# Seven half-size block products instead of eight for the two products with w_in, and a second stage that goes part by part

## The chip, the cores and the metric

The kernel runs on one core of a Trainium2 chip. The metric is the device time of one execution in microseconds; the time of a version is the median of its runs. A profile is one execution taken by the hardware profiler: its span goes from the first to the last instruction.

The core has five engines with in-order queues: TensorE (PE; its weight loads are listed apart as PEld), VectorE (DVE), ScalarE (ACT), GpSimd (POOL) and SyncE (SP), whose queue issues all the DMAs here. Matmuls write to PSUM, eight banks of 512 f32 columns; DVE and ACT read them out.

## The reference

Four batches of 576 tokens go through three layers. Cut to what matters:

```python
x = attention(q, k, v)             # 4 x 576 x 512: windows of 32 keys, half of the heads dilated
xk, xr = mix(x, mu_k), mix(x, mu_r)                # with the token before
x = sigmoid(xr @ w_r) * (relu(xk @ w_k) ** 2 @ w_v)
# the second stage:
h = relu(x @ w_in)                                 # 512 -> 1024
u, v = h[..., :512], h[..., 512:]
v_n = (v - mean(v)) / sqrt(var(v) + 1e-6)          # over the 512 channels
v_s = einsum('ts,bsd->btd', w_spatial, v_n) + b_spatial[:, None]
out = (u * v_s) @ w_out
```

All of it is f32. The weights of the layers arrive as 64-bit words and are turned into f32 by two passes on ACT and two on DVE for each chunk of 128 x 512.

## The kernel before

**Split products.** PE multiplies f32 in one pass only in a type that keeps fewer bits (fp32r). Each operand is therefore split: a copy rounded to fp32r (the high part, names in h) and the rest (the low part, names in l). A product is three matmuls into one PSUM group, high x high, high x low and low x high. The function `halves` adds the two operations of a split: the copy (ACT or DVE) and the subtraction (DVE or POOL). The products of batch 0 with w_k are plain f32 instead, one matmul each.

**Staging.** The first stage holds attention and the first mixture for the four batches; `moe1_k`, `moe1_r` and `moe1_v` are its three products, in halves of 288 tokens. Its result x of a batch lies with channels on the partitions, four chunks of 128 channels (`xs[b]`). The second stage is `moe2(b, base)`, once for each batch, one batch after the other:

- x2: x is split into x2h and x2l, eight pieces of 288 tokens.
- vt: v for 128 tokens at a time, tokens on the partitions, 512 channels wide: 4 chunks x 3 matmuls of 512 columns. The 64 tokens that are left over (576 = 4 x 128 + 64) of two batches are put together to one piece of 128 (eh, el). Then relu, statistics, normalization, split into vh and vl (vx for the left-over).
- u: channels on the partitions, 8 groups of 288 tokens: 4 chunks x 3 matmuls of 288 columns each, then a relu out of PSUM.
- sp: the spatial product, 8 groups of 14 matmuls of 288 columns; DVE adds b_spatial (`bb`), POOL multiplies by u, and the result is split into gh and gl.
- out: 128 tokens at a time, 12 matmuls of 512 columns, a copy (`ot`) and a store.

**Memory.** Tiles live in pools. Pool w1 holds w_k and w_r, wv holds w_v, mp the operands of the first stage; all three close before pool p2 (second stage) opens, once the last product of the first stage is read. Pool w2 opens when attention is done and holds the w_in parts (`wi`) and the landing buffers.

**Order.** Nothing is issued as it is written. A planner (`Plan`) gathers the operations with their reads, writes and an assumed cost on each engine that could do them, lays them out in time by a priority and prints the order. The priority is a due time (`plan.at`) plus numbers from a table `TUNE`, kept for each step and kind of result. So each engine's instruction order is fixed when the kernel is built, and the engine of a split too.

All instructions carry the line of the planner's wrapper (L436), so the profile's rows are told apart by tile names.

Of the kernel before, what the change touches and what calls it, by code (L numbers as in the profile page):

```python
# [9 lines left out]
F32 = mybir.dt.float32  # L10
# [26 lines left out]
def blocks(dil):  # L37
# [36 lines left out]
    ('out', 0): {'egh': (-18004, -2638, 792, 0), 'egl': (-6718, -1987, -600, -300), 'ot': (-15781, 3792, 1500, 22), 'out': (-5671, 1120, 792, 22), 'psB': (-7310, 5704, 792, 22)},  # L74
    ('out', 1): {'egh': (-264, -4319, 400, -300), 'egl': (13285, -949, 1500, 2000), 'ot': (10019, 11028, -600, 22), 'out': (16522, -18977, 792, 22), 'psB': (2377, 4422, 792, 22)},
    ('out', 2): {'egh': (8560, -4302, -600, -800), 'egl': (3087, 6359, 400, 2000), 'ot': (8350, 2986, 792, 22), 'out': (31073, 12833, 792, 22), 'psB': (-1776, -9158, 792, 22)},
    ('out', 3): {'egh': (-7306, 7539, 1500, 300), 'egl': (-7842, 6171, 0, 2000), 'ot': (1321, -651, 1500, 22), 'out': (9708, 3552, 792, 22), 'psB': (2644, 6787, 792, 22)},
# [23 lines left out]
    ('soft', 3, 0): {'mx': (1192, -7718, 792, 22), 'psS': (149, 4109, 792, 22), 'psT': (4080, 3666, 792, 22), 'sm': (8575, -3406, 792, 22)},  # L101
# [4 lines left out]
    ('start',): {'ident': (5243, -7493, 792, 22), 'identb': (-2035, 973, 792, 22), 'pt': (7412, 207, 792, 800), 'xok': (11235, 2251, 792, 22)},  # L106
# [16 lines left out]
    ('val', 2, 1): {'psT': (-2551, -876, 792, 22), 'x': (-10263, -5137, 0, 22)},  # L123
    ('val', 3, 1): {'psT': (-2074, 10315, 792, 22), 'x': (-194, -1787, -600, 22)},
# [26 lines left out]
    ('ws',): {'bb': (418, -110, 792, 22), 'psB': (-3423, 1530, 792, 22), 'raw2': (-8052, 4304, 792, 22), 'wsh': (-6574, 2299, -200, 22), 'wsl': (11527, -6628, 792, 22), 'wslz': (-14987, 3682, 792, 22), 'wst': (-1771, 1627, 792, 22)},  # L151
# [296 lines left out]
def kernel(  # L448
# [54 lines left out]
    enter("one", "w1")  # L503
# [35 lines left out]
    pool_of = {}  # L539

# [11 lines left out]
    def chunk(key, x):  # L552

        k = (key, x)
        if k not in tiles:
            home, tag = key, x
            if key[0] in WHOLE and x == 1:
                home, tag = before(key), 2
            if home is None:
# [13 lines left out]
    def split_weight(pool_name, src, rows, cols, name, raw_of, nraw, tmp_of, ntmp, order, step=0, lead=0, room=()):  # L573
# [5 lines left out]
        for j, (c0, r) in enumerate((c0, r) for c0 in range(0, cols, CH) for r in range(rows)):  # L579
# [20 lines left out]
            def load(e, kr=kr, r=r, c0=c0):  # L600
                nc.sync.dma_start(raw_of(kr), s[:, r, 2 * c0 : 2 * (c0 + CH)])

            def words(kr=kr):
                w2 = raw_of(kr).rearrange("p (n t) -> p n t", t=2)
                return w2[:, :, 0], w2[:, :, 1]
# [40 lines left out]
            if not whole:  # L646
                split(key, number, tk, room)
# [1180 lines left out]
```

## Time and profile before

| | us |
|---|---|
| device time, median of 3 runs | 595.57 |
| lowest and highest run | 594.42, 597.0 |
| span of the profiled execution (its device time is not given apart from the runs) | 593.8 |
| busy in it: PE, DVE, ACT, POOL | 571.2, 372.2, 279.7, 125.5 |
| mean granted TensorE clock | 0.993 of full speed |
| second stage (first u product to last out product) | about 375 to 590 |

The busy time of an engine is the time in which at least one of its instructions runs; matmuls overlap, so their mean durations add up to more than PE's busy time. Idle time of an engine that nobody waits for costs nothing.

### The profile page before, as it was taken

Reading aid. Unit: us, or ns where it says so; the run is one execution under the profiler, and the core shown is the slowest. Engines: PE = TensorE matmul, PEld = TensorE weight load, DVE = VectorE, ACT = ScalarE, POOL = GpSimd, SP = SyncE. Lnnn points to the kernel's source line nnn. Section 1 sums busy time; section 2 is a strip of 40 time slices with the busy share of each in tenths; the row PEclk is TensorE's granted clock in tenths of the full one; section 3 lists DMA queues with packets and bytes.
Section 4 is the critical chain, followed back from the end, with each engine's and each line's share of the span. In section 5 each row is a group of like instructions: output and inputs, shape, how many; then the busy total and the mean of one; then the engine's idle time right before and its main releaser. Section 6 shows DMA issues by size and latency. Waiting matters only on the chain.

```text
span 593.8 us, 13602 instructions
## 1 busy us (share of the span) xinstructions
PE 571.2 (96%) x5595; PEld 525.1 (88%) x5595; DVE 372.2 (63%) x785; ACT 279.7 (47%) x700; POOL 125.5 (21%) x149
## 2 busy tenths in 40 slices
PE   9798999997989999999999999999999999999997
PEld 7666788797978999999999999889998998898995
DVE  6698999887889564682598830579835206534340
ACT  3578987694345271354649561256324312312322
POOL 1022401730244111120134200101400801420030
PEclk9899999998999999999999999999999999999999
DMA  9879662526656102000023300121001001101002
GB/s 256 228 175 191 182 173 45 89 72 136 106 127 126 21 29 64 1 2 1 1 92 126 109 2 24 45 84 47 25 19 55 2 18 48 25 0 72 1 0 90
DMA packets 90942, 43.13 MB, mean 73 GB/s; under 512 B 77120, under 2 KB 83264, under 8 KB 90880
## 3 DMA queue, kind: packets, MB, share of 16 engines
q1 hardware_dynamic: 90880, 42.26, 28.4%
q8 instruction: 44, 0.72, 0.5%
q14 instruction: 18, 0.15, 0.1%
HBM read 37.52 MB, written 4.72 MB: 71 GB/s over the span
## 4 chain that ended last, share of the span: by engine, by line
PE 82%; DVE 7%; issue 4%; ACT 4%; SPq 2%; DMA 1%; POOL 1%; DVEq 0%; POOLq 0%; ACTq 0%
PE psM L436 55%; PE psB L436 17%; PE psT L436 7%; PE psS L436 2%; SPq L436 2%; DVE tmp L436 1%; DVE st L436 1%; DVE wk L436 1%; ACT kr L436 1%; DVE xm L436 1%; DVE temps L436 1%; ACT pt L436 1%; DMA ld<-in_k_dram 0%; DMA ld<-in_q_dram 0%; ACT pr L436 0%
## 5 line engine op out<-in xcount | busy, mean ns | idle before, releaser
L436 PE MATMUL psM<-xh,wk 128*128 128x288 f32 x512 | 116.5, 325 | 0.8 <-DVE x L436 0.5
L436 PE MATMUL psM<-sq_dt.float32r,wv 128*128 128x288 f32 x768 | 113.7, 300 | 1.4 <-DVE x L436 0.7
L436 PEld LDWEIGHTS psM<-sq_dt.float32r,wv 128*128 128x128 f32 x768 | 105.5, 190 | 3.5 <-ACT x L436 1.5
L436 PEld LDWEIGHTS psM<-xh,wk 128*128 128x128 f32 x512 | 87.0, 188 | 8.1 <-DVE x L436 0.8
L436 PE MATMUL psM<-xh,wr 128*128 128x288 f32 x256 | 59.6, 300 | 1.1 <-DVE kr L436 0.9
L436 PE MATMUL psM<-xl,wk 128*128 128x288 f32 x192 | 56.6, 295 | 0.0
L436 PE MATMUL psM<-x2h,wi 128*128 128x288 f32 x256 | 55.0, 296 | 0.0
L436 POOL TENSOR_TENSOR g<-g,u 128x288 f32<-128x288 f32 x32 | 27.4, 869 | 109.3 <-DVE g L436 109.3
L436 PEld LDWEIGHTS psM<-xh,wr 128*128 128x128 f32 x256 | 43.6, 188 | 2.5 <-DVE kr L436 1.2
L436 PEld LDWEIGHTS psM<-x2h,wi 128*128 128x128 f32 x256 | 42.4, 188 | 1.1 <-ACT u L436 0.5
L436 ACT ACTIVATE kr<-psM 128x288 f32<-128x288 f32 x52 | 21.1, 406 | 43.8 <-PE psM L436 42.0
L436 POOL TENSOR_TENSOR xl<-xm,xh 128x288 fp32r<-128x288 f32 x24 | 24.0, 1005 | 80.0 <-DVE xh L436 62.6
L436 PE MATMUL psB<-wi,x2h 128*128 128x512 f32 x128 | 40.3, 396 | 0.0
L436 PE MATMUL psB<-wo,gh 128*128 128x512 f32 x128 | 39.7, 391 | 0.0
L436 PE MATMUL psM<-x2l,wi 128*128 128x288 f32 x128 | 38.0, 297 | 0.8 <-DVE x2l L436 0.8
L436 PE MATMUL psM<-xl,wr 128*128 128x288 f32 x128 | 37.9, 296 | 0.5 <-POOL xl L436 0.5
L436 PE MATMUL psM<-wsh,vh 128*128 128x288 f32 x128 | 37.8, 296 | 0.1
L436 PE MATMUL psM<-wsl,vh 128*128 128x288 f32 x128 | 37.7, 295 | 0.0
L436 PE MATMUL psM<-wsh,vl 128*128 128x288 f32 x128 | 37.7, 295 | 0.0
L436 POOL TENSOR_TENSOR pr<-pr,st 128x384 f32<-128x384 f32 (+1 forms) x22 | 20.3, 925 | 77.0 <-DVE st L436 72.8
L436 DVE SCALAR_TENSOR_TENSOR xm<-xd,mu,x 128x288 f32<-128x288 f32 x56 | 33.9, 620 | 3.9 <-POOL xl L436 3.7
L436 PEld LDWEIGHTS psM<-xl,wk 128*128 128x128 f32 x192 | 36.1, 188 | 0.3 <-POOL xl L436 0.3
(165 smaller groups left out, 1194.4 us busy)
## 6 DMA issues: line engine op xcount, KB each, us to landing
vw<-in_v_dram SPq DMA_DIRECT2D x36, 128.0 KB, 3.0
room<-in_moe_w_k_dram SPq DMA_DIRECT2D x8, 512.0 KB, 5.8
room<-in_moe_w_v_dram SPq DMA_DIRECT2D x8, 512.0 KB, 4.1
raw<-in_moe_w_in_dram SPq DMA_DIRECT2D x8, 512.0 KB, 3.7
out_dram<-ot SPq DMA_DIRECT2D x16, 256.0 KB, 2.0
ld<-in_k_dram SPq DMA_DIRECT2D x48, 72.0 KB, 3.2
ld<-in_q_dram SPq DMA_DIRECT2D x48, 72.0 KB, 2.5
vw<-in_v_dram SPq DMA_DIRECT2D x16, 144.0 KB, 4.8
```

Source lines behind the costliest of these rows:

```text
L436: return self.tc.keep_in_program_order(getattr(self.engine, name)(*args, **kw))
```

## The change

Both products with w_in are done for the first 512 tokens of a batch by a scheme of seven products of half-size blocks where eight would be plain. The 512 input channels, the 512 output channels and the 512 tokens are each cut in two halves of 256. From the four blocks of a weight half (u or v) come seven weight blocks (11, S1, S2, S3, 12, S4, 22), four of them by adding or subtracting; from the four blocks of x come seven input blocks (11, T2, T1, T3, 21, 22, T4). All 14 + 7 blocks are split into high and low parts. One block product (`times`) is 2 x 2 x 3 = 12 matmuls of 256 columns into one bank; the results are put together by a copy (`keep`) and seven additions from PSUM (`join`) in each of u and v. u is written over `xs[b]`, v into `vr[b]`. The input blocks have one set of buffers.

The 64 tokens left over of two batches are done apart (`tails`), from the same weight blocks: for v with 256 columns, for u with 128 columns.

The stage now goes part by part: u and v for all four batches (`split_x`, `seven`), then for each batch the spatial product and the out product (`finish`). relu is applied to v in memory and to u in the gating, which moves from POOL to DVE. The spatial product is cut at token 256 instead of 288. Pool w1 stays open to the end, and its rooms (w_k, w_r) take the v weight blocks, input blocks, g and w_out; w_out is loaded after the u weights' rooms are free. TUNE has new numbers for all steps that changed and for the last two batches of the first stage.

```diff
-    split_weight("w2", w_in, NC, DF, "wi", ...
+    BL = ("11", "S1", "S2", "S3", "12", "S4", "22")
...
+        block(0, lambda: n(0, 0), k(0))
+        change(0, lambda: n(1, 0), lambda: n(1, 1), ALU.add, k(0) + k(1))
+        block(1, wt[0], [("wt", 0)])
+        change(0, wt[0], lambda: n(0, 0), ALU.subtract, k(0) + [("wt", 0)])
+        block(2, wt[0], [("wt", 0)])
+        change(1, lambda: n(0, 0), lambda: n(1, 0), ALU.subtract, k(0))
+        block(3, wt[1], [("wt", 1)])
+        block(4, lambda: n(0, 1), k(1))
+        change(0, lambda: n(0, 1), wt[0], ALU.subtract, k(1) + [("wt", 0)])
+        block(5, wt[0], [("wt", 0)])
+        block(6, lambda: n(1, 1), k(1))
...
+                (place("w1", tag, [P, 2, MD], F32R, f"wv2_{i}_{x}"), room_after(keys))
+                for x, (tag, keys) in enumerate(wk_rooms[2 * i : 2 * i + 2])
...
+    STEPS = (("11", "11"), ("S2", "T2"), ("S1", "T1"), ("S3", "T3"), ("12", "21"), ("S4", "22"), ("22", "T4"))
...
+        for x_ in ("v", "u"):
+            ps, key = spare_bank()
+            for half in range(2):
+                def emit(e, x_=x_, half=half, ps=ps):
+                    todo = list(terms(x_, half))
+                    for m in range(1 if x_ == "v" else 2):
+                        for j, (nm, k_, th, tl) in enumerate(todo):
+                            wh, wl = (blocks_[x_, nm][y]()[:, k_] for y in range(2))
+                            first, last = j == 0, j == len(todo) - 1
+                            if x_ == "v":
+                                out_ = ps()[:, half * MD : (half + 1) * MD]
+                                three = ((th(), wh), (th(), wl), (tl(), wh))
+                            else:
+                                m0 = (2 * half + m) * P
+                                out_ = ps()[:, m0 : m0 + P]
+                                ms = slice(m * P, (m + 1) * P)
+                                three = ((wh[:, ms], th()), (wh[:, ms], tl()), (wl[:, ms], th()))
...
+        block("11", lambda: x(0, 0), g(0, 0))
+        change(0, lambda: x(0, 1), lambda: x(0, 0), g(0, 1))
+        block("T1", wt[0], [("wt", 0)])
+        change(0, lambda: x(1, 1), wt[0], g(1, 1) + [("wt", 0)])
+        block("T2", wt[0], [("wt", 0)])
+        change(1, lambda: x(1, 1), lambda: x(0, 1), g(0, 1) + g(1, 1))
+        block("T3", wt[1], [("wt", 1)])
+        block("21", lambda: x(1, 0), g(1, 0))
+        block("22", lambda: x(1, 1), g(1, 1))
+        change(0, wt[0], lambda: x(1, 0), g(1, 0) + [("wt", 0)])
+        block("T4", wt[0], [("wt", 0)])
...
+        banks = [near("psM" if x_ == "u" else "psB", i) for i in range(3)]
...
+                for m in range(2):
+                    o = view(ps)[:, m]
+                    ms = slice(m * P, (m + 1) * P)
+                    for k_ in range(2):
+                        for q, (a, c) in enumerate(((0, 0), (0, 1), (1, 0))):
+                            nc.tensor.matmul(
+                                o, l[a][:, k_, ms], r[c][:, k_],
+                                start=k_ == 0 and q == 0, stop=k_ == 1 and q == 2,
+                            )
...
+        a, b_, c = banks
+        times(0, a)
+        keep(a, 0, 0)
+        times(1, b_)
+        join(b_, 0, 1, 0, 0)
+        times(2, c)
+        times(3, a)
+        join(a, 1, 0, 0, 1)
+        join(c, 0, 1, 0, 1)
+        join(c, 1, 1, 1, 0)
+        times(4, b_)
+        join(b_, 0, 0, 0, 0)
+        times(5, a)
+        join(a, 0, 1, 0, 1)
+        times(6, c)
+        join(c, 1, 0, 1, 0, ALU.subtract)
...
+    for b in range(B):
+        base = 10000 + 400 * b
+        if b % 2 == 0:
+            tails(b, base - 300)
+        split_x(b, base - 250)
+        seven(b, "u", base)
+        seven(b, "v", base)
...
+        ends = (slice(0, MD), slice(MD, S))
...
+                def gate(e, g=g, o=o, hf=hf):
+                    nc.vector.scalar_tensor_tensor(
+                        g()[:, :MD], xs[b][:, o, MD * hf : MD * (hf + 1)], 0.0, g()[:, :MD],
+                        op0=ALU.max, op1=ALU.mult,
+                    )
...
     for b in range(B):
-        moe2(b, 10000 + 1000 * b)
+        finish(b, 12000 + 500 * b)
```

## Rows read from the trace of the kernel before

**Rows 1.** The page, busy us of each engine, share of the span, instructions:
```profile
PE 571.2 (96%) x5595; PEld 525.1 (88%) x5595; DVE 372.2 (63%) x785; ACT 279.7 (47%) x700; POOL 125.5 (21%) x149
```

**Rows 2.** Busy us by stretch: length, PE, PEld, DVE, ACT, POOL; PEclk, DMA share, GB/s:
```profile
355.00:375.00 20.00, 19.50 (x147) 19.21 (x145) 2.71 (x6) 6.02 (x17) 1.57 (x2) 1.00 0.08 19
375.00:590.00 215.00, 213.37 (x1292) 193.70 (x1290) 106.14 (x238) 69.23 (x153) 43.48 (x52) 1.00 0.10 35
```

**Rows 3.** What PE waited for from 375 to 594 us: total us, times, longest:
```profile
PE psM L436 <- DVE x2l L436: 0.8, 1, 0.8
```

**Rows 4.** Groups by form, from 375 to 590 us (busy us, mean ns), and by tile wi:
```profile
L436 PE MATMUL psM<-x2h,wi 128*128 128x288 f32 x256 | 55.0, 296 | 0.0
L436 PE MATMUL psB<-wi,x2h 128*128 128x512 f32 x128 | 40.3, 396 | 0.0
...
L436 PE MATMUL psB<-wi,el x8: 389/390/397, 389.9 to 489.8; 128*128 128x512 f32 x8
```

**Rows 5.** PE in order of time: start us, us, instructions merged in a row:
```profile
384.21 0.29 PE L436 MATMUL psM<-x2l,wi 128*128 128x288 f32 x1
...
385.00 0.29 PE L436 MATMUL psM<-x2l,wi 128*128 128x288 f32 x1
...
389.91 0.40 PE L436 MATMUL psB<-wi,el 128*128 128x512 f32 x1
...
391.99 0.39 PE L436 MATMUL psB<-wi,el 128*128 128x512 f32 x1
```

**Rows 6.** The same for 128 columns, weight loads, plain f32, and one transpose's duration:
```profile
380.99 0.71 PE L436 MATMUL psB<-ident,raw 128*128 128x128 f32 x5
...
L436 PE MATMUL psB<-ident,raw x25: 221/272/273, 381.0 to 394.1; 128*128 128x128 f32 x20, 64*128 64x64 f32 x5
...
381.43 0.19 PEld L436 LDWEIGHTS psM<-x2h,wi 128*128 128x128 f32 x1
381.54 0.19 PEld L436 LDWEIGHTS psM<-x2l,wi 128*128 128x128 f32 x1
...
59.74 5.58 PE L436 MATMUL psM<-xh,wk 128*128 128x288 f32 x22
```

**Rows 7.** DVE in order of time, from 376 to 421 us:
```profile
376.70 1.93 DVE L436 TENSOR_TENSOR x2l<-x,x2h 128x288 fp32r<-128x288 f32 x5
...
411.34 0.68 DVE L436 TENSOR_TENSOR wo<-tmp,wo 128x512 fp32r<-128x512 f32 x1
411.94 0.68 DVE L436 SCALAR_TENSOR_TENSOR tmp<-tmp,raw 128x512 uint32<-128x512 uint32 x1
...
420.55 1.29 DVE L436 TENSOR_TENSOR wo<-tmp,wo 128x512 fp32r<-128x512 f32 x1
```

**Rows 8.** Groups by form of POOL and DVE (busy us, mean ns | idle before):
```profile
L436 POOL TENSOR_TENSOR g<-g,u 128x288 f32<-128x288 f32 x32 | 27.4, 869 | 109.3 <-DVE g L436 109.3
...
L436 POOL TENSOR_TENSOR pr<-pr,st 128x512 f32<-128x512 f32 x5 | 5.6, 1118 | 33.6 <-DVE st L436 30.5 <-ACT pr L436 3.2
...
L436 DVE BATCH_NORM_STATS2 bn<-vt 128x6 f32<-128x512 f32 x18 | 12.5, 692 | 14.1 <-ACT vt L436 14.0
...
L436 DVE TENSOR_SCALAR vt<-vt,mv 128x512 f32<-128x512 f32 x18 | 9.7, 542 | 0.5
...
L436 DVE TENSOR_SCALAR u<-psM 128x288 f32<-128x288 f32 x11 | 5.0, 457 | 7.9 <-PE psM L436 7.8
...
L436 DVE BATCH_NORM_AGGREGATE mv<-bn 128x2 f32<-128x6 f32 x18 | 3.3, 182 | 0.6
L436 DVE RECIPROCAL mv<-mv 128x1 f32<-128x1 f32 x18 | 2.8, 156 | 2.7 <-ACT mv L436 2.6
```

**Rows 9.** Tiles wk and wv: count, ns min/median/max, first and last start in us:
```profile
L436 PE MATMUL psM<-xh,wk x512: 288/295/510, 42.5 to 355.1; 128*128 128x288 f32 x171
...
L436 PE MATMUL psM<-sq_dt.float32r,wv x768: 288/294/587, 78.6 to 375.0; 128*128 128x288 f32 x192
```

**Rows 10.** DMA issues: count, KB each, median us to landing:
```profile
raw<-in_moe_w_out_dram SPq DMA_DIRECT2D x4, 512.0 KB, 3.6
```

More of the change, by code (lines that the diff above doesn't have):

```diff
@@ L502 @@
     enter("all", "psM", space=PSUM)
-    enter("one", "w1")
+    enter("keep", "w1")
     enter("one", "mp")
@@ L638, in upper @@
-            def upper(e, number=number, words=words):
-                u = number().bitcast(U32)
-                nc.vector.scalar_tensor_tensor(
-                    u, words()[1], 0x80000000, u, op0=ALU.bitwise_and, op1=ALU.bitwise_or
-                )
-            add({"dve": dve(CH)}, lower, r=[tk, rk, yk], w=[tk], two=True)
-            add({"dve": dve(CH)}, upper, r=[tk, rk], w=[tk], two=True)
+            convert(s, name, r, c0, raw_of, rk, number, tk, order, lead, room if whole else ())
@@ L646, in split_weight, with convert, load, words @@
             if not whole:
                 split(key, number, tk, room)
+    def convert(s, name, r, c0, raw_of, rk, number, tk, order, lead, room=()):
+        kr = rk[1]
+        def load(e):
+            nc.sync.dma_start(raw_of(kr), s[:, r, 2 * c0 : 2 * (c0 + CH)])
+        def words():
+            w2 = raw_of(kr).rearrange("p (n t) -> p n t", t=2)
+            return w2[:, :, 0], w2[:, :, 1]
+        plan.tag = ("w", name, "ld")
+        add({"dma": packets(P, 4096)}, load, w=[rk], r=order, lat=2000, at=plan.at - lead)
+        plan.tag = ("w", name)
+        add(
+            {"act": act(CH) + 60},
+            lambda e: nc.scalar.activation(
+                number(), words()[1].bitcast(F32), AF.Abs, scale=2.0**-112
+            ),
+            r=[rk, *room], w=[tk],
+        )
+        yk = ("low", rk)
+        add(
+            {"act": act(CH) + 60},
+            lambda e: nc.scalar.activation(
+                words()[0], words()[0], AF.Copy, bias=-0.499, scale=2.0**-29 * (1 - 2.0**-12)
+            ),
+            r=[rk], w=[yk],
+        )
+        def lower(e):
+            u = number().bitcast(U32)
+            nc.vector.scalar_tensor_tensor(
+                u, u, 3, words()[0], op0=ALU.logical_shift_left, op1=ALU.bitwise_or
+            )
+        def upper(e):
+            u = number().bitcast(U32)
+            nc.vector.scalar_tensor_tensor(
+                u, words()[1], 0x80000000, u, op0=ALU.bitwise_and, op1=ALU.bitwise_or
+            )
+        add({"dve": dve(CH)}, lower, r=[tk, rk, yk], w=[tk], two=True)
+        add({"dve": dve(CH)}, upper, r=[tk, rk], w=[tk], two=True)
@@ L1147, in halves @@
             lambda e: two(e, lo(), src(), f32(hi()), ALU.subtract),
-            r=list(src_keys) + [hk], w=[lk], two=True,
+            r=list(src_keys) + [hk], w=[lk], two=True, after=after[1],
         )
@@ L1431, in open_p2, with place, at, t2 @@
         enter("three", "p2", reuse_waits="tile")
+    def place(pool_name, tag, shape, dtype, name, part=None):
+        def at():
+            if name not in tiles:
+                tiles[name] = pools[pool_name].tile(shape, dtype, tag=tag, name=name)
+            return tiles[name] if part is None else tiles[name][:, part]
+        return at
+    def t2(shape, dtype, name):
+        return lambda: get("p2", shape, dtype, name)
+    firsts = [(("wk", r, c0), ("wk_%d_%d_0" % (r, c0), "wk_%d_%d_2" % (r, c0))) for c0 in (0, CH) for r in range(NC)]
@@ new lines, with room_after @@
+    wk_rooms, lo_tag = [], "spare"
+    for key, (hi_tag, whole_tag) in firsts:
+        wk_rooms.append((hi_tag, [(key, 0)]))
+        wk_rooms.append((lo_tag, [(key, 1)]))
+        lo_tag = whole_tag
+    wk_last = (lo_tag, [("whole", firsts[-1][0])])
+    wr_rooms = [("wr_%d_0_%d" % (r, x), [(("wr", r, 0), x)]) for r in range(NC) for x in range(2)]
+    def room_after(keys):
+        return users_of([k for k in keys if k in plan.written])
+    BL = ("11", "S1", "S2", "S3", "12", "S4", "22")
@@ new lines, with numbers @@
+    s_in = w_in.bitcast(U32).rearrange("(r p) c -> p r c", p=P)
+    raw2 = lambda i: get("w2", [P, 2 * CH], U32, f"raw2_{i}")
+    wt = [place("w2", f"wt{i}", [P, 2, MD], F32, f"wt{i}") for i in range(2)]
+    blocks_ = {}
+    num_ = place("w2", "num", [P, NC, CH], F32, "num")
+    num = {"u": num_, "v": num_}
+    vr = [num_] + [t2([P, NC, DM], F32, f"v{b}") for b in range(1, B)]
+    def numbers(x, c0, at):
+        for r in range(NC):
+            plan.at = at
+            sk = plan.slot("raw2", 2)
+            convert(
+                s_in, "wi" + x, r, c0, raw2, ("raw2", sk),
+                lambda x=x, r=r: num[x]()[:, r], ("num", r), ["w2"], 0,
+            )
@@ new lines @@
+    none = set()
+    numbers("u", 0, 4905)
+    weight_blocks(
+        "u",
+        [
+            [(place("w2", f"wu{i}", [P, 2, 2, MD], F32R, f"wu{i}", x), none) for x in range(2)]
+            for i in range(7)
+        ],
+        4906,
+    )
+    numbers("v", CH, 4907)
+    weight_blocks(
+        "v",
+        [
+            [
+                (place("w1", tag, [P, 2, MD], F32R, f"wv2_{i}_{x}"), room_after(keys))
+                for x, (tag, keys) in enumerate(wk_rooms[2 * i : 2 * i + 2])
+            ]
+            for i in range(7)
+        ],
+        8300,
+    )
@@ L1457, with spare_bank, near, spatial @@
     add({"dve": 70}, lambda e: nc.vector.memset(zero(), 0.0), r=["p2"], w=["zero"])
+    def spare_bank():
+        sk = 3 + plan.slot("psBs", 2)
+        return (lambda: get("psB", [P, 512], F32, f"psB{sk}")), ("psB", sk)
+    def near(kind, sk):
+        if kind == "psM":
+            return (lambda: get("psM", [P, 512], F32, f"psM{sk}")), ("psM", sk)
+        return (lambda: get("psB", [P, 512], F32, f"psB{sk}")), ("psB", sk)
     wsh = t2([P, NT + 1, S], F32R, "wsh")
     wsl = t2([P, NT + 1, S], F32R, "wsl")
-    for t in range(NT + 1):
-        plan.at = 9141
+    def spatial(t):
         plan.tag = ("ws",)
@@ new lines, in split_x, with block, change @@
+    def split_x(b, base):
+        plan.at = base
+        plan.tag = ("x2", b)
+        x = lambda i, j: xs[b][:, 2 * i : 2 * i + 2, MD * j : MD * (j + 1)]
+        g = lambda i, j: [("g", b, c, h) for c in (2 * i, 2 * i + 1) for h in range(j + 1)]
+        def block(nm, src, keys):
+            h, l = X[nm]
+            halves(
+                src, h, l, 2 * MD, keys + (["p2"] if nm in XB[4:] else ["w2"]),
+                ("X", nm, 0), ("X", nm, 1), after=x_room[nm],
+            )
+        def change(t, a, b_, keys):
+            add(
+                {"dve": dve(2 * MD), "pool": pool(2 * MD)},
+                lambda e: two(e, wt[t](), a(), b_(), ALU.subtract),
+                r=["w2", *keys], w=[("wt", t)], two=True,
+            )
+        block("11", lambda: x(0, 0), g(0, 0))
[9 more added lines that the diff above has]
+        block("T4", wt[0], [("wt", 0)])
@@ L1507 @@
+    plan.at = 9141
+    for t in range(NT + 1):
+        plan.at = 9141 + 300 * t
+        spatial(t)
+    plan.tag = ("ws",)
     add(
@@ new lines, in free, with pair @@
+    def free(pool_name, tag, shape, dtype, name, keys, part=None):
+        return place(pool_name, tag, shape, dtype, name, part), users_of(keys)
+    def pair(nm, block):
+        return [(nm, block, x) for x in range(2)]
+    v_home = {}
+    for t in range(NT):
+        for x in range(2):
+            if t < 2:
+                keys = [("raw2", t), ("wst", t, 0), ("wst", t, 1), ("low", ("raw2", t))]
+                v_home[0, t, x] = free("w2", f"raw2_{t}", [P, 2, DM], F32R, f"vA{t}", keys, x)
+            else:
+                i = 2 * (t - 2) + x
+                v_home[0, t, x] = free(
+                    "w1", wr_rooms[i][0], [P, DM], F32R, f"vA{t}_{x}", [("X", XB[i // 2], i % 2)]
+                )
+            v_home[1, t, x] = free("w2", f"wu{t}", [P, 2, DM], F32R, f"vB{t}", pair("wu", BL[t]), x)
@@ new lines @@
+    g2 = [single([P, S - MD], F32, f"g2{d}") for d in range(2)]
+    wo_users = set()
+    for r in range(NC):
+        for x in range(2):
+            tag, keys = left.pop(0)
+            homes[("wo", r, 0), x] = ("w1", tag)
+            wo_users |= users_of(keys)
+    egs = [single([P, NC, 2, LR], F32R, f"eg{'hl'[x]}") for x in range(2)]
+    xroom = lambda i: [("X", XB[i // 2], i % 2)]
+    vtmp, vx0, vx1, ot0, ot1 = [
+        free("p2", f"X{i}", [P, DM], d, nm, xroom(i))
+        for i, d, nm in ((8, F32R, "vtmp"), (9, F32R, "vx0"), (10, F32R, "vx1"), (11, F32, "ot0"), (12, F32, "ot1"))
+    ]
@@ new lines @@
+    vx, ots = (vx0, vx1), (ot0, ot1)
+    plan.at = 11300
+    for i in range(2):
+        plan.written["roomw", i] = users_of(pair("wu", BL[4 + i]))
+    plan.written["roomt"] = users_of(pair("wu", BL[6]))
+    plan.written["roomo"] = wo_users
+    s_out = w_out.bitcast(U32).rearrange("(r p) c -> p r c", p=P)
+    raw3 = lambda i: place("w2", f"wu{4 + i}", [P, 2 * CH], U32, f"raw3_{i}")()
+    pool_of["wo"] = "w1"
+    for r in range(NC):
+        kr, kt = plan.slot("raw3", 2), plan.slot("num3", 2)
+        number = place("w2", "wu6", [P, 2, CH], F32, "num3", kt)
+        convert(
+            s_out, "wo", r, 0, raw3, ("raw3", kr), number, ("num3", kt), [("roomw", kr)], 0, ["roomt"]
+        )
+        split(("wo", r, 0), number, ("num3", kt), ["roomo"])
@@ new lines, in finish @@
+                lambda t=t: vr[b]()[:, t], h, l, DM, [("v", b, t)], ("vh", b % 2, t), ("vl", b % 2, t),
+                after=(ha, la),
+            )
+        if even:
+            plan.tag = ("vx", b)
+            v_ = vtl[b // 2]
+            tmp, ta = vtmp
+            add(
+                {"act": act(DM), "dve": dve2(DM)}, lambda e: copy(e, tmp(), v_()),
+                r=[("vtl", b // 2)], w=["vtmp"], two="both", after=ta,
+            )
+            for d in range(2):
+                rows = slice(d * LR, (d + 1) * LR)
+                o, oa = vx[d]
@@ L1650, in moe2 @@
+                    r=["vtmp"], w=[("vx", d, 0)], two="both", after=oa,
+                )
+                add(
+                    {"dve": dve(DM), "pool": pool(DM)},
+                    lambda e, o=o, rows=rows: two(
+                        e, o()[LR:], v_()[rows], f32(tmp()[rows]), ALU.subtract
+                    ),
+                    r=[("vtl", b // 2), "vtmp"], w=[("vx", d, 1)], two=True, after=oa,
+                )
+        ends = (slice(0, MD), slice(MD, S))
         for o in range(NC):
@@ L1717, in moe2 @@
-        plan.at = base + 740
-        plan.tag = ("out", b)
-        for eg, g, nm in ((egh, gh, "gh"), (egl, gl, "gl")):
-            add(
-                {"act": act(NC * LR), "dve": dve(NC * LR), "pool": pool(NC * LR)},
-                lambda e, eg=eg, g=g: copy(e, eg()[:, :, b % 2], f32(g()[:, :, NT * P :])),
-                r=[(nm, c, 1) for c in range(NC)], w=[("e" + nm, b % 2)], two="both",
-            )
+                    lambda g=g: g()[:, :MD],
+                    lambda gh=gh, hf=hf: gh()[:, MD * hf : MD * (hf + 1)],
@@ L1780 @@
             plan.ops[i][1](e)
-    for g in ("three", "two", "all"):
+    for g in ("three", "two", "keep", "all"):
         stacks[g].close()
```

473 lines of the change are left out of this document (256 added, 217 removed), and 81 rows, old and new, of the table TUNE.

## Prediction

> **What bounds the kernel now.** I read the page first [rows 1]: TensorE (PE) is busy for 571.2 us, 96% of the span, VectorE (DVE) for 372.2. A share over the whole span says little about one stage, so the next view was the busy time by stage [rows 2]. The change lies almost wholly in the second stage, from 375 us to 590. There PE is busy 213.4 of 215 us at a granted clock of 1.00, DVE 106.1. The waits of that stretch confirm it [rows 3]: PE waits once, 0.8 us, for a split of the stage's input. The reader is to see that this stage lasts as long as its matmuls, that nothing can be won in it but matmul time, and that half of DVE is free there to pay with.
>
> **Removed and added matmuls.** The two products with w_in form six groups now: 256 + 128 = 384 matmuls of 288 columns for u, 128 + 64 + 16 + 8 = 216 of 512 columns for v (one of u, one of v and the smallest stand in [rows 4]). Matmuls overlap, so the mean duration of one is not its price; the spacing of starts is. Between 384.21 and 385.00 us lie six steps of 288 columns, 0.132 us each; between 389.91 and 391.99 us nine of 512, 0.231 us each [rows 5]. Now: 384 x 0.132 + 216 x 0.231 = 50.7 + 49.9 = 100.6 us.
>
> After: seven block products of 12 matmuls with 256 columns, for u and for v, over four batches, make 672. The tails (the last 64 tokens of two batches) bring 2 x 24 matmuls of 256 columns for v and 2 x 48 of 128 columns for u. So 600 matmuls become 816, with fewer columns in all.
>
> No matmul of this split type (fp32r) has 256 columns in the trace. The line through 288 and 512 has 0.099/224 = 0.00044 us a column and gives 0.118 us. Bounds: 0.107, which is 256/288 of the 120 ns that 288 columns need at the 2.4 GHz clock granted here, and 0.132, the 288 row itself if a shorter one is no cheaper. I take the line: 720 x 0.118 = 85.0 us (77 to 95).
>
> The 96 matmuls of 128 columns are the disputed term. The line gives 0.061 us. But each needs its own weight load, and right after a run of transposes two loads of the split type start at 381.43 and 381.54 us, 0.11 us apart, with no long stream between them [rows 6]. The transposes there, also 128 columns over 128 x 128 weights, step by (0.71 - 0.27)/4 = 0.11 us too. The upper end is plain f32: batch 0's w_k products with 288 columns step by (5.58 - 0.30)/21 = 0.25 us and take two records each (512 records [rows 9] for 448 products), which is 0.22 us for 128 columns. I take 0.11, the row of the same tile and the same loads: 96 x 0.11 = 10.5 us; the ends are 5.9 and 21.
>
> Sum: 85.0 + 10.5 = 95.5 against 100.6, a gain of 5.1 us (9.7 and a loss of 5.4 with the ends of the disputed term). The cut of the spatial products into 256 and 320 columns costs nothing by the line: 0.118 + 0.146 = 2 x 0.132. With 256 columns at 0.132 it costs 224 x 0.014 = 3.1 us. The out products and the transposes of w_spatial keep their number and size.
>
> **What the vector engines get.** A DVE pass over 512 columns costs 0.60 us back to back (411.34 to 411.94), over 288 columns 0.39 us (five in 1.93 us) [rows 7]. While GpSimd (POOL) works, one at 420.55 needs 1.29 us.
> - Each batch has 14 joins (DVE adds from PSUM): 56 x 0.60 = 33.6 us, new. The copies out of PSUM for u and v that they replace lay mostly on ScalarE (ACT).
> - Four differences and seven low parts of the input per batch: 44 x 0.60 = 26.4 us, where 32 passes of 288 columns stood (32 x 0.39 = 12.5 us, part of them on POOL).
> - Gating moves from POOL, 32 x 0.87 us [rows 8], to DVE: 32 passes of 0.39 plus small ones, some 14 us.
> - The weights need six more splits and eight differences: 14 x 0.60 = 8.4 us.
> - Less: the relus of u that DVE did, 5.0 us [rows 8].
>
> So DVE takes on 33.6 + 13.9 + 14 + 8.4 - 5.0, some 65 us, in a stage where it had 109 us free. That is hidden on average. It isn't spread evenly, though. The u and v part of all batches now lasts 85.0 + 10.5 + 2.5 (transposes) = 98 us on PE. DVE's work that belongs to it is 33.6 + 26.4 + 18 normalizations of 1.57 (statistics 0.69 + 0.18, reciprocal 0.16, scaling 0.54 [rows 8]), 28.3 + some 11 for w_spatial and the tails (estimated from as many passes of 0.60) = 99 us, if none goes to POOL or later. The normalization of batches 1 to 3 (14 of 18, 22 us) is only needed by the spatial part, and POOL can take differences and low parts at 1.12 us for 512 columns [rows 8]. With that and ten such passes on POOL (6 us) DVE stands near 71 of 98 us: covered, with less room than now. In the spatial part, 109 us on PE, DVE has some 16 us per 27 us batch. Covered.
>
> **New waits.**
> - The first copy out of PSUM of u in a batch writes over that batch's x, so it waits until all 14 input parts are written; the last of these waits for the last u and v product of the batch before. Behind it, in ACT's or DVE's queue, stand the joins, and PE's fourth product needs their banks. PE has six products first (three banks each for u and v): 6 x 12 x 0.118 = 8.5 us. The late work is one copy (0.6), one low part (0.6) and what stands ahead in the queue (four joins, 2.4): 3.6 us. Hidden; without that cover every microsecond late costs one.
> - At the change of stages the v weights take the rooms of w_k, whose last use is at 355.1 us; PE then has w_r and w_v until 375.0 [rows 9]. In these 20 us DVE is busy 2.7 and ACT 6.0 [rows 2]. To be fitted in: 11 DVE passes and 7 ACT copies for the weights, 7 and 4 for the first input blocks, some 3 us of tails: 14 us of DVE. It fits if little of it is late. The input parts 21, 22 and T4 live in memory that opens only at 375 us: 4 passes and 3 copies, near 3.5 us, against the same 8.5 us of cover.
> - w_out is loaded after the u weights are done with: SP's queue holds its four loads behind that wait, and the stores come later anyway. Landing takes 3.6 us [rows 10], a chunk's conversion some 4 us, four chunks through two rooms some 12 us. The cover is the first batch's spatial products, 56 x (0.118 + 0.146) = 14.8 us, with 3 us to spare. DMA is not what is short: the u weights' loads keep their place, and those of w_spatial are only spaced out.
>
> All of this is hidden on paper, through in-order queues and banks that come round after three products. The stage now waits 0.8 us; I put 2.5 us more on it (bounds 0 and 10, the price of rival B).
>
> **Sum.** 593.8 (span) - 5.1 + 2.5 = 591.2. The profiled execution's own time isn't given; the three runs' median, 595.6, stands 1.8 us above its span. So 593.0 us.
>
> **Rule against trace.** The starts show the pair of load and stream for 288 columns at 0.132 us, where 288 columns alone need 0.120: the load is hidden [rows 5]. The Trainium skill, "TensorE: Matmul & The Clock Gate", section "The mechanism" of its Part 3, says that a weight load overlaps running matmuls only if it goes to other rows of the array; all loads here fill all 128 rows. By that rule every load would stand in the open, and 216 more of them would make the change a loss. The trace disagrees with that rule, at 288 and at 512 columns.
>
> **Rivals.**
> - A, narrow matmuls at the plain f32 rate. 96 x 0.22 = 21 us instead of 10.5. For it: the type has never run below 288 columns here. Against: the transposes with 128 columns do 0.11. Time 593.0 + 10.5 = 603.5, slower; by more than 0.5% from 0.17 us on. 15%.
> - B, DVE becomes the bound of the u and v part. For it: 99 us of work against 98, with PSUM banks waiting for joins, and 1.29 us passes beside POOL. Against: what can go to POOL and to later. If PE loses a tenth of that part, 9.8 us instead of 2.5: 600.3. 17%.
> - C, narrow matmuls on the line at 0.061 us: 593.0 - 4.6 = 588.4. Against it: the loads 0.11 us apart. 13%.
> - D, 256 columns no cheaper than 288 (0.132): 10.1 + 3.1 us more, 606.2. Against: 512 and 288 lie on a line that leaves room. 5%.
> - E, the weight loads of the added matmuls aren't hidden: 216 x 0.11 = 23.8 us, against 24576 columns fewer (221184 now, 196608 after), 24576 x 0.00044 = 10.8 us: 595.6 + 13.0 = 608.6. Against: the 0.132 us step of 288 columns. 2%. It is what the rule quoted above would make of the change.
> - The forecast, narrow at 0.11 with 0 to 6 us of waits: 590.5 to 596.5. 48%.
>
> **Numbers.** 0.5% is 3 us, about what a measurement of this kernel can tell from no change. Faster than 592.6: half of the forecast (0.24) and all of C (0.13), together 0.37. Slower than 598.5: A but for its edge (0.14), D and E (0.07) and six tenths of B (0.10), together 0.31. Same: the rest, 0.32. The range 588 to 604 leaves out D, E, half of A (0.07) and less than half of C (0.05), 0.19 in all. The forecast's own range is 590.5 to 596.5.
>
> **What would show it.** In the changed profile, starts of 256-column matmuls near 0.118 us and of 128-column ones near 0.11; the last out product some 3 us earlier; DVE near three quarters busy in the u and v part; PE's waits in the second stage, for joins or input parts, below 4 us in all. Wrong would be the forecast if the 128-column tails step by 0.2 us, if the waits on DVE run to 10 us, or if the switch near 375 us shows a gap.

## The result, and the profile after

| | before | after |
|---|---|---|
| median of the runs | 596.2 us (594.42 to 597.0, 4 runs) | 589.51 us (589.1 to 589.94, 4 runs) |
| ratio | | 0.9899, 95% interval 0.9879 to 0.992 |
| profiled execution: span | 593.8 us | 588.0 us (own time 589.94) |

The kernel is 1.0% faster, 6.7 us. The forecast was 593.0 with a range of 588 to 604, and 590.5 to 596.5 for the likeliest case alone: the result is inside the first and 1 us below the second. One execution in all the experiments below (608.39 us, first stage's old entries) lay more than 1.5% above the fastest of its kernel; the ratios leave it out.

The page of the changed kernel, busy time of each engine; it answers to [rows 1]:
```profile
PE 568.1 (97%) x5811; PEld 530.8 (90%) x5811; DVE 420.8 (72%) x865; ACT 282.3 (48%) x689; POOL 176.9 (30%) x190
```
PE does 216 more instructions in 3.1 us less. DVE took on 48.6 us, POOL 51.4. The stretches of [rows 2], after:
```profile
355.00:375.00 20.00, 20.00 (x156) 19.96 (x155) 12.19 (x18) 7.25 (x16) 8.51 (x7) 1.00 0.01 2
375.00:590.00 215.00, 208.29 (x1500) 197.91 (x1498) 140.02 (x306) 74.44 (x153) 66.35 (x67) 0.99 0.12 38
```
The 0.8 us that PE waited for in the second stage [rows 3] are gone, and nothing came in their place: the list of PE's waits from 375 us on is empty. All but 0.3 us of PE's idle time in the second line lies behind the last product, which starts at 583.2 us, 5.7 us earlier than before:
```profile
583.20 0.39 PE L459 MATMUL psB<-wo,egl 128*128 128x512 f32 x1
```
```profile
588.94 0.39 PE L436 MATMUL psB<-wo,egl 128*128 128x512 f32 x1
```

The new groups of matmuls by form, from 375 to 590 us (busy us, mean ns | idle before):
```profile
L459 PE MATMUL psB<-wv,X 128*128 128x256 f32 x331 | 42.8, 283 | 0.0
L459 PE MATMUL psM<-X,wu 128*128 128x256 f32 x312 | 39.7, 281 | 0.1
...
L459 PE MATMUL psB<-eh,wu 128*128 128x128 f32 x48 | 8.6, 273 | 0.0
```
Their price is the spacing of starts. PE in order of time (start us, us, matmuls merged in a row):
```profile
395.94 2.99 PE L459 MATMUL psM<-X,wu 128*128 128x256 f32 x24
...
418.38 0.38 PE L459 MATMUL psB<-eh,wu 128*128 128x128 f32 x2
418.61 0.28 PE L459 MATMUL psB<-el,wu 128*128 128x128 f32 x1
418.72 0.38 PE L459 MATMUL psB<-eh,wu 128*128 128x128 f32 x2
```
24 matmuls of 256 columns take 2.99 us, the last of them 0.28 from its start: (2.99 - 0.28)/23 = 0.118 us. Three of 128 columns lie between 418.38 and 418.72 us: 0.11 us each, hardly less than for twice the columns. Over the whole trace the mean spacing of starts is 0.119 us for 256 columns and 0.111 for 128.

### The profile page after: what moved, and what is told of

Read it like the earlier page. It is cut to its first block, busy times and chain, and to the rows that moved or that the text cites. A ratio compares the mean times of both kernels' runs of the same rounds, so it can differ in the third digit from the quotient of the medians.

```text
span 588.0 us, 14180 instructions
## 1 busy us (share of the span) xinstructions
PE 568.1 (97%) x5811; PEld 530.8 (90%) x5811; DVE 420.8 (72%) x865; ACT 282.3 (48%) x689; POOL 176.9 (30%) x190
## 4 chain that ended last, share of the span: by engine, by line
PE 78%; DVE 11%; issue 3%; DMA 2%; ACT 2%; SPq 1%; POOL 1%; DVEq 0%; POOLq 0%; ACTq 0%
PE psM L459 52%; PE psB L459 16%; PE psT L459 7%; PE psS L459 2%; DVE num L459 2%; DMA ld<-in_k_dram 1%; DVE x L459 1%; SPq L459 1%; DVE v L459 1%; DVE g L459 1%; DVE sq_dt.float32r L459 1%; DVE pt L459 1%; DVE kT L459 1%; ACT pt L459 1%; DVE temps L459 1%
## 5 line engine op out<-in xcount | busy, mean ns | idle before, releaser
L459 PE MATMUL psM<-xh,wk 128*128 128x288 f32 x512 | 117.8, 327 | 0.5 <-DVE x L459 0.4
L459 PE MATMUL psB<-wv,X 128*128 128x256 f32 x336 | 43.4, 283 | 0.0
L459 PE MATMUL psM<-X,wu 128*128 128x256 f32 x336 | 42.8, 280 | 0.1
L459 PEld LDWEIGHTS psB<-wv,X 128*128 128x128 f32 x336 | 41.2, 190 | 0.1
L459 PEld LDWEIGHTS psM<-X,wu 128*128 128x128 f32 x336 | 40.8, 188 | 0.3 <-DVE x L459 0.3
L459 ACT ACTIVATE kr<-psM 128x288 f32<-128x288 f32 x48 | 19.5, 407 | 37.8 <-PE psM L459 36.8
L459 DVE TENSOR_TENSOR x<-psM,x 128x288 f32<-128x288 f32 x32 | 14.3, 451 | 24.4 <-PE psM L459 22.4
L459 POOL TENSOR_TENSOR sq_dt.float32r<-kr,sq_dt.float32r 128x288 fp32r<-128x288 f32 x24 | 22.6, 946 | 25.8 <-DVE sq_dt.float32r L459 16.8
L459 POOL TENSOR_TENSOR gl<-g,gh 128x256 fp32r<-128x256 f32 x23 | 18.6, 817 | 37.9 <-ACT gh L459 22.7
L459 PE MATMUL psT<-const-bfloat16-1.0 128*128 128x224 bf16 x224 | 28.3, 282 | 0.8 <-PEq L2151 0.8
```

What stands on the lines that cost most here:

```text
L459: return self.tc.keep_in_program_order(getattr(self.engine, name)(*args, **kw))
```

## Experiments

Each was timed beside the kernel before the change; ratios are to that kernel, the changed kernel's being 0.9899. The code shows the decisive lines alone; three dots stand for the rest.

**The changed kernel again, and an eighth product.** The first is the same program. In the second the 12 matmuls of each first block product are issued twice, 96 more of 256 columns; the repeat starts the accumulation anew, so the output is the same.
```diff
-                for m in range(2):
+                for m in list(range(2)) * (2 if n == 0 else 1):
```


> The changed kernel once more, beside the others on the same chip: 589.5 us, 1.0% below the kernel before. All theories expect that; it is the base for the next three.

> The matmuls of the first block product are issued twice (the second time gives the same result again), with the instruction order as it was: 96 more matmuls of 256 columns, as many as a plain scheme of eight products would have. Theory (the stage lasts as long as its matmuls): 96 x 0.119 = 11.4 us more, 600.9 us, slower than the kernel before. Rival (DVE sets the pace in the u and v part, PE only follows): the added matmuls fall into time that PE has anyway, 590 to 595 us.

Again: 589.8 us (588.84 to 590.22), ratio 0.9911 (0.9883 to 0.9939), no wait of PE after 360 us. Eight products: 600.1 us (599.0 to 600.7), ratio 1.0082 (1.005 to 1.0115), as the theory said. 96 x 0.118 = 11.3 us more of matmuls cost 10.3 to 10.6 us. PE's time sets the stage's end. With eight products the kernel is 5 us slower than before: the smaller blocks by themselves lose (in this order, which was made for seven), and the gain is the eighth product left out.

**Narrow matmuls narrower still.** The u tails as 192 matmuls of 64 columns in place of 96 of 128.
```diff
-                    for m in range(1 if x_ == "v" else 2):
+                    for m, ds in ((0, None),) if x_ == "v" else [
+                        (m, slice(d * LR, (d + 1) * LR)) for m in range(2) for d in range(2)
+                    ]:
...
```


> The 128-column matmuls of the u tails are cut in two of 64 columns each, 192 instead of 96, with all else as it was. Theory (a narrow matmul costs its weight load, 0.11 us, however few columns follow): 192 x 0.11 = 21.1 us instead of 10.6, 600 us, and starts 0.11 us apart in the profile. Rival (narrow matmuls of this type take two cycles for a column, which at 128 columns is also 0.107 us): 192 x 0.055, no change, 589.5 us, and starts 0.055 us apart.

613.79 us (613.03 to 614.06), ratio 1.0313 (1.028 to 1.0345): 24 us more, beyond both. PE in order of time, where these matmuls begin and in the second of the two tails:
```profile
416.93 0.39 PE L459 MATMUL psB<-eh,wu 128*128 128x64 f32 x2
417.16 0.28 PE L459 MATMUL psB<-el,wu 128*128 128x64 f32 x1
417.27 0.39 PE L459 MATMUL psB<-eh,wu 128*128 128x64 f32 x2
...
443.28 0.61 PE L459 MATMUL psB<-eh,wu 128*128 128x64 f32 x2
443.70 0.40 PE L459 MATMUL psB<-el,wu 128*128 128x64 f32 x1
443.92 0.61 PE L459 MATMUL psB<-eh,wu 128*128 128x64 f32 x2
```
The first steps settle the question between the two: three in 0.34 us, 0.11 each, as with twice the columns. At 64 and at 128 columns a step costs the 0.11 us at which two weight loads came in [rows 6]. That it is the load that sets this floor fits, but no run tells it apart from another fixed cost of a matmul. Later three take 0.64 us, 0.21 each. The busy time by stretch (PE the second column, PEclk the third from the end) says why:
```profile
422.00:426.00 4.00, 4.00 (x22) 4.00 (x22) 0.00 (x0) 0.00 (x0) 0.00 (x0) 0.53 0.00 0
...
434.00:438.00 4.00, 4.00 (x29) 4.00 (x28) 2.47 (x3) 0.62 (x1) 0.80 (x1) 0.77 0.01 4
438.00:442.00 4.00, 4.00 (x39) 4.00 (x38) 0.00 (x0) 0.00 (x0) 0.00 (x0) 1.00 0.00 0
442.00:446.00 4.00, 4.00 (x24) 4.00 (x24) 0.00 (x0) 0.00 (x0) 0.00 (x0) 0.59 0.00 0
...
454.00:458.00 4.00, 4.00 (x20) 4.00 (x20) 0.00 (x0) 0.59 (x1) 0.00 (x0) 0.50 0.00 0
```
PE is busy throughout, and the granted clock falls to 0.50, the 1.2 GHz level, in both tails, from about 422 to 436 and from 442 to 459 us: some 30 us in which nearly half of the time is lost, 15 us. With the 96 added matmuls, 96 x 0.11 = 10.6, that is roughly the 24 us.

**Four batches' u tails at once.** 48 matmuls of 256 columns in place of 96 of 128, which should save 4.9 us; `eh` and `el` hold four batches, in the rooms of the raw spatial weights.
```diff
-        if b % 2 == 0:
-            tails(b, base - 300)
+        if b == 0:
+            tails(base - 300)
...
-    eh = place("w1", e_rooms[0][0], [P, NC, 2, LR], F32R, "eh")
+    eh = place("w2", "raw2_0", [P, NC, B, LR], F32R, "eh")
...
```


> The left-over tokens of all four batches are taken together for u: 48 matmuls of 256 columns instead of 96 of 128. Their input parts move to the rooms of the w_spatial landing buffers, so they come after w_spatial. Theory: 48 x 0.119 = 5.7 us instead of 10.6, 4.9 us less, 584.6 us, if no new wait appears. Rival (the order was made for two tails, and the one tail now needs all its parts at once): waits of PE of 2 to 8 us on the input parts or on the two PSUM banks, 587 to 593 us.

602.11 us (599.71 to 603.94), ratio 1.0116 (1.0085 to 1.0146). PE's waits from 360 us on (total us, times, longest):
```profile
PE psM L459 <- DVE g L459: 4.7, 6, 1.3
PE psB L459 <- DVE wsl L459: 3.9, 4, 2.6
PE psB L459 <- ACT wsh L459: 2.1, 1, 2.1
```
The priorities were those of the other order, and 12.5 us of waits (four smaller ones with these) outweigh the 4.9. Between these waits the granted clock fell as well, so that PE's busy time is only 0.5 us below the changed kernel's and not 4.9:
```profile
380.00:400.00 20.00, 16.10 (x119) 15.05 (x118) 17.54 (x34) 7.89 (x17) 7.13 (x6) 0.91 0.23 61
400.00:420.00 20.00, 16.97 (x129) 16.47 (x128) 16.56 (x37) 7.50 (x17) 5.29 (x5) 0.91 0.00 1
```
That left open whether the rooms or the order made them. So the second stage's priorities were made anew for these steps, by a search over the planner's own estimate:

> The u tails of all four batches in 48 matmuls of 256 columns instead of 96 of 128, as in the run that took 602 us, but with priorities of the second stage made anew for these steps. Theory (the 12.5 us of waits in that run were those of an order made for other steps): the waits go and 4.9 us of matmuls are saved, 584.5 to 588 us. Rival (the tails of all batches can't start until the last batch's gated values are there, and their rooms bind the transposes of the spatial weights, whatever the order): 593 us and more, the waits for these tiles still in the list.

588.27 us (587.97 to 589.37), ratio 0.9902 (0.9879 to 0.9924). PE is busy for 564.0 us, 4.1 less than in the changed kernel; waits for wsl shrink from 3.9 to 1.1 us, all waits from 375 us on from 12.5 to 2.9. They were mostly a matter of order: the rival falls, and the theory's range is missed by 0.3 us. The time can't be told from the changed kernel's: some 3 us of waits eat most of the saving. A last run tried to win those too, with new priorities for the first stage's batches 2 and 3 (the second stage's were made anew with them):

> As the run with the u tails of all four batches and new priorities for the second stage (588.3 us, TensorE busy for 4.1 us less than in the changed kernel, but idle for some 3 us between 375 and 590 us); here the first stage's steps of batches 2 and 3 get new priorities too, so that the two stages' orders fit each other. Theory (those 3 us are a matter of order): 584.5 to 587 us, TensorE idle for at most 1 us in the second stage. Rival (they belong to the rooms that the tails of four batches must wait for): 588 us and more, with waits for the low parts of the spatial weights (wsl) again. A third case, that the new order disturbs the first stage, would show as more TensorE waits before 360 us than the changed kernel's.

595.59 us (593.81 to 600.59), ratio 1.002 (0.9994 to 1.0046): the third case. PE is idle for 18.7 us before 360 us, 15.2 in the changed kernel. The busy time up to 360 us and from there on, first of the run before, then of this one (PE second):
```profile
0.00:360.00 360.00, 345.15 (x4200) 317.94 (x4202) 274.44 (x553) 205.57 (x531) 97.02 (x113) 0.99 0.41 97
360.00:600.00 240.00, 218.87 (x1564) 207.06 (x1563) 151.70 (x328) 68.80 (x148) 69.21 (x72) 1.00 0.11 34
```
```profile
0.00:360.00 360.00, 341.28 (x4134) 312.20 (x4136) 263.15 (x526) 208.87 (x537) 88.77 (x104) 0.98 0.41 97
360.00:600.00 240.00, 228.76 (x1630) 215.84 (x1628) 171.66 (x359) 76.41 (x164) 64.75 (x59) 1.00 0.11 34
```
At 360 us this run has 66 more matmuls to do than the one before it, 9.9 us of PE's time, and between the two spans lie 9.3: the whole loss is in the first stage, the second isn't worse. Only 3.9 us of it are idle time of PE there; for the rest PE was busy longer for the same matmuls, and why stays open. So does whether the 3 us can be won.

**u tails by tokens.** Tokens on the partitions, as for v, and the result turned by PE.
```diff
-                                three = ((wh[:, ms], th()), (wh[:, ms], tl()), (wl[:, ms], th()))
+                        for q, (l_, r_) in enumerate(((th(), wh), (th(), wl), (tl(), wh))):
...
+                        nc.tensor.transpose(ps()[:, cs], flat()[:, cs], ident[:, :])
...
```


> The u tails are computed as the v tails are, with the tokens on the partitions, and then turned by TensorE: 96 matmuls of 128 columns (96 x 0.11 = 10.5 us) give way to 48 of 256 (48 x 0.118 = 5.7 us) and 8 plain f32 transposes of 0.22 to 0.27 us (2.0 us), with one more copy of 512 columns per pair of batches. The second stage's priorities are made anew for it. Theory (TensorE bounds the stage, an order made for the steps hides the waits): 2.8 us less than the changed kernel, 586 to 588.5 us. Rival (TensorE's free order is a lucky one, any other brings waits): 590 to 598 us with the waits in the list.

590.29 us (588.71 to 592.12), ratio 0.9937 (0.9912 to 0.9962). Matmul work fell a little more than the 2.8 us reckoned (PE busy 564.6, 3.5 us less), and 2.3 us of waits came from 375 us on with the new order. The theory's range is missed: its upper end is 588.5, and the fastest execution took 588.71. The rival's begins at 590 and has the waits. No gain is shown.

**More work for DVE.** First 24 joins twice, then the 18 statistics passes too. I reckoned 14.4 and 26.8 us more; DVE's busy time rose by 16.3 and 29.6 (437.1 and 450.4 against 420.8).
```diff
-                lambda e: two(e, room(i, j), room(i2, j2), view(bank[0]), op),
+                lambda e: [
+                    two(e, room(i, j), room(i2, j2), view(bank[0]), op)
+                    for _ in range(1 if (i, j) == (i2, j2) else 2)
+                ],
...
             nc.vector.bn_stats(st(), v())
+            nc.vector.bn_stats(st(), v())
```


> In the u and v products 24 of the VectorE additions that write a result beside the one they read are issued twice; the second gives the same values, so the output stays as it is. That is 24 x 0.60 = 14.4 us more of VectorE, half of it in the products of batches 0 and 1 (380 to 420 us), half in those of 2 and 3 (440 to 478 us), where VectorE has about 4 and 2 us free. Theory (TensorE bounds the stage and runs ahead on other ready work; the 12 free us of VectorE at 420 to 440 us and the 9 at 478 to 520 us take up the rest): 589.5 to 592 us, hardly a TensorE wait. Rival (VectorE is all but the bound of the u and v products, so what is beyond its free time there goes to the end): 14.4 less 6 = 8 us more, 597 to 599 us, with TensorE waiting for the additions.

> As the run before it, and the 18 statistics passes of the v normalisation are issued twice as well (same result): 14.4 + 18 x 0.69 = 26.8 us more of VectorE in 380 to 540 us, where it is free for 32 us of 160. Theory (hidden until VectorE's free time is used up): the free time is not all at the right place, so 592 to 600 us, the waits in the second group of products and the spatial products behind them. Rival (VectorE all but the bound): some 20 us more, 608 to 612 us.

602.08 us (600.73 to 603.94), ratio 1.0113 (1.007 to 1.0156); and 615.06 us (612.13 to 616.36), ratio 1.0332 (1.029 to 1.0374). My theory fell in both, and the loss goes beyond the rival too: 12.3 and 25.3 us, against 589.8 for the changed kernel. The busy time of the u and v part in the changed kernel (after the length, the pairs are PE, PEld, DVE, ACT, POOL):
```profile
380.00:400.00 20.00, 19.91 (x169) 19.67 (x169) 18.23 (x34) 11.95 (x23) 12.20 (x10) 1.00 0.20 52
400.00:420.00 20.00, 20.00 (x169) 19.60 (x168) 17.77 (x38) 6.64 (x15) 2.29 (x2) 1.00 0.04 10
420.00:440.00 20.00, 20.00 (x175) 20.00 (x175) 7.46 (x15) 4.90 (x10) 1.84 (x2) 1.00 0.00 1
440.00:460.00 20.00, 20.00 (x172) 20.00 (x171) 17.95 (x35) 10.68 (x22) 12.78 (x10) 1.00 0.00 1
```
and, with the 24 joins twice, PE's longest wait and what followed it:
```profile
PE psM L459 <- DVE x L459: 6.8, 4, 2.6
```
```profile
476.00:478.00 2.00, 1.35 (x12) 1.15 (x10) 1.97 (x4) 0.00 (x0) 0.20 (x1) 1.00 0.53 121
478.00:480.00 2.00, 0.09 (x1) 0.09 (x1) 1.97 (x6) 0.29 (x1) 0.00 (x0) 0.81 0.85 242
480.00:482.00 2.00, 2.00 (x8) 2.00 (x9) 1.97 (x6) 0.24 (x2) 0.00 (x0) 0.50 0.40 162
...
486.00:488.00 2.00, 2.00 (x19) 2.00 (x18) 1.71 (x3) 0.49 (x1) 0.00 (x0) 0.98 0.00 0
```
DVE has 4 of 40 us free in the first pair's products. The 12.5 free us at 420 to 440 us don't help: more than half of PE's work there is tails, which don't wait for joins, and in the fixed order the products behind a late join wait in PE's queue. There are 8.8 us of waits from 375 us on, and after the longest the clock is 0.50 for 6 us of busy matmuls, some 3 us more. With both additions the waits from 375 us on are 19.2 us. How much of it an order made for the longer joins would win back wasn't tried.

**Priorities.** The changed kernel without entries for the second stage's steps; then with the first stage's old entries; then the kernel before without entries for its second stage. One line of each kind stands for the others:
```diff
-    ('u2', 0): {'cu': (-41869, -3118, -200, 800), 'psM': (-56981, -24374, 200, 800)},
...
-    ('v', 3, 1): {'g': (-14757, -29339, 792, -300), 'psM': (-17631, -41623, 200, 2000)},
+    ('v', 3, 1): {'g': (-10024, -3296, 792, 22), 'psM': (-8118, -2527, 792, 22)},
```

> The table of priorities has no entries for the second stage's steps: the same instructions there, in the order that the planner gives by the steps' due times alone. Theory (the waits that I priced at 2.5 us, with a bound of 10, are there when a group of products follows its own joins, and the priorities put other work between): TensorE waits 5 to 15 us between 375 and 590 us, 595 to 605 us. Rival (so much independent work is ready that the order hardly matters): within 2 us, 588 to 591.5 us.

> The first stage's steps (k, r and v of the batches 1 to 3) get back the priorities that they had before the change; nothing else differs. Theory (part of the gain, some 1.8 us of fewer TensorE waits before 375 us, comes from the order of the first stage and not from the products): 591 to 592 us, the waits back before 375 us. Rival (those waits differ from run to run, all of the gain is in the second stage): 589 to 590 us.

> The kernel before the change, whose table of priorities has no entries for the second stage's steps (the counterpart of the changed kernel without them, which took 599.0 us). Theory (the gain is the matmul work, the order only has to hide waits in either kernel): it loses about as much as the changed kernel did, 9.5 us, so 603 to 607 us, and the split is worth some 6 us with or without priorities. Rival (the split is worth nothing by itself and the gain is a better order): 595 to 600 us, no more than the changed kernel without priorities.

Changed kernel without: 599.01 us (596.7 to 601.84), ratio 1.0066 (1.0037 to 1.0094). PE waits from 375 us on, first the longest:
```profile
PE psB L420 <- ACT gh L420: 5.4, 1, 5.4
PE psB L420 <- DVE v L420: 0.8, 1, 0.8
```
8.3 us in all. Time and waits are as large as the theory said, but its cause holds for little of them: the longest wait is for the split of the gated values (gh), not for joins. Behind it the clock is at half again:
```profile
488.00:490.00 2.00, 0.00 (x0) 0.00 (x0) 1.97 (x7) 0.91 (x2) 0.00 (x0) 0.71 0.00 0
490.00:492.00 2.00, 1.26 (x3) 0.79 (x3) 2.00 (x5) 1.05 (x3) 1.24 (x2) 0.50 0.00 0
...
496.00:498.00 2.00, 2.00 (x10) 2.00 (x9) 0.58 (x3) 0.41 (x1) 1.00 (x2) 0.50 0.00 0
```
Kernel before without: 606.75 us (605.36 to 607.27), ratio 1.0206 (1.0179 to 1.0233), with waits for halves of v:
```profile
PE psM L415 <- ACT vh L415: 4.1, 2, 3.5
PE psM L415 <- POOL vl L415: 1.9, 2, 1.1
```
So the second stage's entries are worth 1.7% in the new kernel and 2.1% in the old one. They set more than the order: a split's engine hangs on them too (in the changed kernel DVE is busy for 401.2 us without them and 420.8 with them). Between the two kernels without them the change still wins, 1.0066 against 1.0206, some 8 us, so the gain doesn't come from these entries. But 8 us is more than the matmuls save, so part of it is a matter of the two plans; and each kernel kept its own entries for the first stage.

With the first stage's old entries: 601.79 us (598.02 to 608.39), ratio 1.0105 (1.0065 to 1.0145), neither case. Both stages' steps go through one plan, and in the trace the order of PE's matmuls in the second stage differs from the changed kernel's, so the run doesn't test the first stage alone. Whether the first stage has a share in the gain it doesn't tell.

## Why the prediction was right, and where it was off

- **What bounds the kernel.** Right: 11.3 us more of matmuls cost 10.3 to 10.6.
- **Matmuls of 256 columns.** Forecast 0.118 us, measured 0.118 to 0.119: 720 x 0.119 = 85.7 us against 85.0.
- **The disputed 96 of 128 columns.** Forecast 0.11, measured 0.111: 10.7 us against 10.5. Rivals A and C fall, and the run with 64 columns agrees with the reason that was given, the load: the step stays at 0.11.
- **The spatial products' cut.** Forecast nothing. Measured 0.119 + 0.148 for 256 and 320 columns against 0.264: 224 x 0.003 = 0.7 us. Rival D falls.
- **The sum of the matmuls.** 85.7 + 10.7 + 0.7 - 100.6 = 3.5 us won, 5.1 forecast; PE's busy time fell by 3.1.
- **Added waits: the mis-sized term.** I put 2.5 us more of waits on the second stage (0 to 10). There are none, and the 0.8 us that was there went. Up to its last product PE is idle for 15.5 us, 18.1 before. The rest, 1.8 us, is ahead of 375 us; but with this one first-stage order PE's idle time up to 365 us runs from 12.3 to 16.2 us over six profiles, and the two with the old order have 16.7, so a share of the first stage is neither shown nor excluded. In the spans it is 3.1 + 2.6 = 5.7 of the 5.8 us, against 5.1 - 2.5 = 2.6 forecast.
- **What was luck.** The two errors have opposite signs: the matmuls gave 2 us less than forecast, PE's idle time 5 us more. The 1.8 us ahead of 375 us stand in no term of the forecast. So the direction and the bound were understood; that the time came out so near the forecast is in part luck.
- **Why no waits.** None of the covers that I named gave way, but not because DVE had much room: I reckoned 71 of 98 us, the trace shows 79 from 380 to 478 us and 36 of 40 in the first products (a join took 0.66 us and not 0.60: 18.6 us for the 28 of them in the row below), with POOL busy for 51 us more over the whole trace although its gating had left it; I had moved ten passes to it. The entries for the second stage's steps hide waits: 8.3 us without them. DVE's total was 65 us more by my sum and 49 by the page.
```profile
L459 DVE TENSOR_TENSOR x<-x,psM 128x512 f32<-128x512 f32 x28 | 18.6, 678 | 0.2
```
- **Rival B** was nearer than its 17% says. It needs DVE to be full in the products' own stretch; the 24 joins issued twice make it true, in the order as it was. As built, the change stops just short.
- **Rival E.** The 256-column pairs start 0.118 us apart with a weight load of 128 rows each, so here too the load is hidden. The trace disagrees with the rule of the Trainium skill, "TensorE: Matmul & The Clock Gate", section "The mechanism", that a load overlaps running matmuls only in other rows. The same section also lets a load into a background weight buffer go ahead, which the trace would fit, though it can't show the buffer.

## What to carry to other kernels

Price a matmul by the spacing of starts of the nearest rows. Here the line through 288 and 512 columns held down to 256, but not for narrow ones: at 128 and at 64 columns the step was the 0.11 us at which weight loads followed each other. When an engine bounds a stage at 100%, look at the second engine by stretch and not by stage, and test it by issuing its passes twice: DVE was 65% busy over the stage and yet, in the fixed order, had hardly any room beside the products. Saving matmuls in such a plan isn't enough: with the old priorities 48 fewer cost 12 us, and with new ones the saving could still not be told from nothing. So both kernels of a comparison should be seen without their priorities too.

## What the hardware showed that I had not expected

- The granted clock fell to 0.50 while PE was busy without a gap, in two stretches of matmuls of 64 columns (they begin at 416.8 and 438.2 us), and came back among matmuls of 256 columns. With 128 columns at the same 0.11 us a step it stays at 1.00 (the rows of the changed kernel from 400 to 440 us).
- A wait can cost more than its length. In the changed kernel without the second stage's entries PE was idle for 5.4 us (485.4 to 490.7), and the clock was 0.50 until past 498 us; with the joins twice it was idle for 2.6 us, and the clock was 0.50 until 486. That cost another 3 to 4 us each time. Not every wait does it: one of 2.4 us between 380 and 400 us of the run with the joins twice left the clock at 1.00.
